# Block one of a fused scan, gated unit and squared-ReLU kernel: state copies moved to ScalarE, tiles passed whole, two tiles as three products

## The chip, the cores and the metric

The kernel runs on one core of a Trainium2 chip. The metric is the device time of one launch, in microseconds (us), as the median of three runs. A core has TensorE (PE: matrix products, with its weight loads shown apart as PEld), VectorE (DVE), ScalarE (ACT), GpSimd (POOL), and SyncE (SP), which here only issues transfers. Each engine takes its own instructions strictly in the order in which they were issued to it, and waits on semaphores for the others.

## The reference

Three stages follow each other. A state-space scan over 4 x 8 heads of 768 steps, in chunks, then a gated unit, then a squared-ReLU layer:

```python
# scan, per chunk (log_a is summed within the chunk to cum)
y = (C B^T * exp(cum_i - cum_j) * causal) x + (C state) * exp(cum)
state = exp(sum) * state + sum_j B_j x_j exp(cum_end - cum_j)
# gated unit on 3072 tokens of 256, d_ff 1536
xn = x / sqrt(mean(x * x) + 1e-6) * rms_g
x = (silu(xn @ w_gate) * (xn @ w_val)) @ w_out
# squared ReLU, d_ff 2048
out = (s * relu(x @ w_in) ** 2 + b) @ w_out2
```

## The kernel before

**Work and its names.** The 3072 tokens are 32 *units* of 96 tokens (`UT`), worked on in pairs. For a pair, `scan` spreads the decays over partitions with PE (tile `ab`) and scans them on DVE (`a_sb`), `gram` multiplies B and C on PE (tile `y`) and masks the result on DVE (`m`), `outs` makes y from `m` and `xh` on PE, squares it on ScalarE (`xn`, with its row sums in `ss`), raises the sums to the power -1/2 on GpSimd (`rs`) and scales y on ScalarE (`xn` again), and `turn` transposes `xn` on PE and copies it out, scaled by `rms_g`, as `xth` (and, from block two on, its remainder `xtl`). `keep_state` copies the state rows of a unit (16 x 256) into `xh` of the unit two further on, which needs them for its own y.

**The gated unit** takes the units in seven *blocks*; block one (`j == 0`) is 4 units, 384 columns. The 1536 hidden features are 12 weight tiles (`F1`). Tiles come as the raw words of the array (`raw`) and are decoded to `w1f` by `decode`: on DVE `e`, the masked `raw`, a `SCALAR_TENSOR_TENSOR` into `w1f`, the product of `e` and `sg`, and the last product into `w1f`; on ScalarE `sg` and the exponent `e`. From block two on a product is *three products*: weights and data are split into a high part (`w1h`, `xth`, `hi`: a copy on ScalarE) and the rest (`w1l`, `xtl`, `lo`: a subtraction on DVE), and high*high, low*high, high*low are summed, each a fast pass. Block one has the *plain* form: `hidden1_plain` takes the float32 tile `w1f` as it is, in four-pass products. It does so half by half: half 0 is the columns of the first pair of units, half 1 those of the second pair. Half 0 of tiles runs while the second pair is still in the scan; half 1 follows three tiles behind (`behind`). A half is 4 products into one bank of `h` (gate and value side by side), a Silu on ScalarE, a product on DVE (both into the small tile `h`), and, two halves later (`LAG`), 2 products into the sums `o`.

**What sets the order.** Nothing is issued as it is written. `Plan` records every operation, prices it, schedules it (`forward`, `backward`), and issues each engine's operations in the order of the planned starts. Where the plan has TensorE idle before 34 us (`AWAKE`), `issue` fills the gap with small products of ones (line 354; "fills" below). All other instructions are issued at line 361, so the rows below are told apart by their tiles. Transfers go out on SyncE in the planned order; at most eight are under way.

Of the kernel before, what the change touches and what calls it, by code (L numbers as in the profile page):

```python
# [40 lines left out]
F1 = 12  # L41
F2 = 16
N2 = 512
HALF = N2 // 2
# [13 lines left out]
class Plan:  # L58
# [7 lines left out]
    SEM_OF = {"tensor": 0.26}  # L66
    DMA_LEAD, DMA_TAIL, DMA_ISSUE, DMA_RATE = 1.7, 1.3, 0.55, 270e3
    DMA = {"sync": "dma", "scalar": "dma0"}
# [14 lines left out]
    def __init__(self, nc):  # L83
        self.nc, self.ops, self.clock, self.pace = nc, [], 0.0, False
        self.seen, self.rings, self.masks, self.before, self.heads = {}, {}, {}, {}, {}
        self.closed, self.sent, self.turns, self.bundle = set(), None, False, None
        self.now_free, self.floor, self.latest = True, None, None
        self.fresh, self.after, self.held, self.squares = False, None, None, None
        for e in ("tensor", "vector", "scalar", "gpsimd", "sync"):
            setattr(self, e, Engine(self, e))  # L90
# [76 lines left out]
    def touch(self, op, ap, write):  # L167
        t = getattr(ap, "tensor", None)
        tag = getattr(t, "tag", None)
        if tag is None:  # L170
            return
        tag = str(tag)
        name = ap.name
        whole = "PSUM" in str(ap.space) or "DRAM" in str(ap.space)
        if name not in self.seen:
            self.seen[name] = []
            ring = self.rings.setdefault(tag, [])
            bufs = t.bufs or t.tag_meta.bufs
            self.before[name] = list(self.seen[ring[-bufs]]) if len(ring) >= bufs else []
            self.closed.update(ring[:1 - bufs] if bufs > 1 else ring)  # L180
            ring.append(name)
        for *_, o in self.before[name]:
            self.need(op, o)
        p0, p1, mask = (0, 128, self.banks(ap)) if whole else self.cover(ap)
        for w, q0, q1, m, o in self.seen[name]:
            if (write or w) and q0 < p1 and p0 < q1 and m & mask:
                self.need(op, o)
        assert name not in self.closed, name
        self.seen[name].append((write, p0, p1, mask, op))
# [10 lines left out]
    def price(self, eng, fn, args, kw):  # L200
# [4 lines left out]
        if fn == "dma_start":  # L205
            return max(0.06, out.nbytes() / self.DMA_RATE)
        if eng == "tensor":
# [11 lines left out]
        if eng == "vector":  # L219
# [6 lines left out]
            return (n / (1.92 if fast else 0.96) + 67 + more) / 1e3  # L226
        if fn == "tensor_tensor":
            return 0.9 if self.now_free else 2.0
        return n / 1.15e3 + (0.25 if fn == "affine_select" else 0.06)
# [9 lines left out]
    def forward(self, succs, late):  # L239
# [15 lines left out]
        for _ in ops:  # L255
# [24 lines left out]
            if e in ("dma", "dma0"):  # L280
                done = carried = max(now + self.DMA_LEAD, carried) + op["dur"]
                flights.append(done + 0.85)
# [93 lines left out]
def scan_glu_relu2(ctx: ExitStack, tc: tile.TileContext, bc, xr, aa, cst, w1, w2, gn, sv, bv, out):  # L376
# [33 lines left out]
    warm = const.tile([P, 1], F32, name="warm")  # L410
    held = const.tile([P, NPAIR], F32, name="held")
    a_scr = dram.tile([2 * NUNIT, NH * AW], F32, name="a_scr")

    w1h = [wts.tile([P, 6, P], F32R, tag="w1h", name="w1h") for m in range(F1)]
    w1f, w1l, w2f, w2h = {}, {}, {}, {}
# [157 lines left out]
    def keep_state(c):  # L573
        for z in range(2):
            t = z ^ c % NPAIR
            copy = nc.scalar.copy if c >= NPAIR else nc.vector.tensor_copy
            copy(out=x_t[c + NPAIR][z * R:z * R + NST], in_=rows_of(c)[t * R:t * R + NST])

    def outs(units):
# [28 lines left out]
        nc.gpsimd.tensor_tensor(out=rs, in0=ss, in1=mhalf.to_broadcast([P, NPAIR]), op=ALU.pow)  # L608
        if units[0] == 0:

            nc.vector.tensor_copy(out=held, in_=rs)
            nc.held = len(nc.ops) - 1
        for c in units:
# [20 lines left out]
    def turn(units):  # L634
        for c in units:
            j = BLOCK[c]
            if c == FIRST[j]:
                xt_h[j] = xt_p.tile([P, 2, NB[j]], F32R if j else F32, tag="xth", name="xth")
                if j:
                    xt_l[j] = xt_p.tile([P, 2, NB[j]], F32R, tag="xtl", name="xtl")  # L640
        bundled("t", units, turn_products)
        for c in units:
            j, p = BLOCK[c], c % NPAIR
            step = steps_of(j, p).index(c // NPAIR)
            tp = y_t.pop(c)[:, 1, 4 * R:4 * R + 2 * P].rearrange("p (k z r) -> p k z r", k=2, z=2)
            for k in range(2):
                src = tp[:, k, :, NST:R]
                hi = columns(xt_h[j][:, k], j, p)[:, step]
                nc.scalar.activation(out=hi, in_=src, func=AF.Copy, scale=g_sb[:, k:k + 1])
                if j:  # L650
                    lo = columns(xt_l[j][:, k], j, p)[:, step]
                    nc.vector.scalar_tensor_tensor(
                        out=lo, in0=src, scalar=g_sb[:, k:k + 1], in1=f32(hi), op0=ALU.mult, op1=ALU.subtract
                    )

# [11 lines left out]

    def decode(raw, out, n):

# [16 lines left out]
        )  # L686
        nc.after, nc.held = nc.held, None
        nc.vector.scalar_tensor_tensor(
            out=out, in0=low, scalar=2.0 ** -32, in1=high, op0=ALU.mult, op1=ALU.add
        )  # L690
        pw = e.bitcast(BF16)
        nc.after = None
        nc.vector.tensor_tensor(out=pw, in0=pw, in1=sg, op=ALU.mult)
        nc.vector.tensor_tensor(out=out, in0=out, in1=pw, op=ALU.mult)

# [14 lines left out]
    def decode1(m):  # L710
        if m not in raw1:
            load1(m)
        raw = raw1.pop(m)
        w1f[m] = wlo.tile([P, 6, P], F32, tag="wlo", name="w1f")
        decode(raw, flat(w1f[m]), 6 * P)

    def split1(m):
        w1l[m] = wlo.tile([P, 6, P], F32R, tag="wlo", name="w1l")
        split(flat(w1f.pop(m)), flat(w1h[m]), flat(w1l[m]))


    def decode2(m):
        raw = w2_p.tile([P, 4 * P], I64, tag="w2", name="raw2")
        words(raw, w2[m])
        w2f[m] = w2f_p.tile([P, 4, P], F32, tag="w2f", name="w2f")
        decode(raw, flat(w2f[m]), 4 * P)
        if m:
# [11 lines left out]

    def split(src, hi, lo):  # L740
        nc.scalar.copy(out=hi, in_=src)
        nc.vector.tensor_tensor(out=lo, in0=src, in1=f32(hi), op=ALU.subtract)

# [5 lines left out]
    def out1(j, m, hi, lo):  # L749
        if m == 0:  # L750
            o_t[j, 1] = new_o()
        o = [t[:, :NB[j]] for t in o_t[j, 1]]
        for t in range(2):
            three(o[t], w1h[m][:, 4 + t, :], w1l[m][:, 4 + t, :], hi, lo, m == 0, m == F1 - 1)
            if m == F1 - 1:
                evac1(o, t, j)
# [13 lines left out]
    def hidden1(j, m):  # L770
        gv = []
        for v in range(2):
            ps = ps_h.tile([P, 512], F32, tag="h", name="h")[:, :NB[j]]
            for k in range(2):
                three(ps, w1h[m][:, 2 * k + v, :], w1l[m][:, 2 * k + v, :],
                      xt_h[j][:, k], xt_l[j][:, k], k == 0, k == 1)
            gv.append(ps)
# [8 lines left out]
    def hidden1_plain(j, m, half):  # L786
        n = NB[j] // 2
        cols = slice(half * n, (half + 1) * n)
        ps = ps_h.tile([P, 512], F32, tag="h", name="h")[:, :2 * n].rearrange("p (v n) -> p v n", v=2)
        for v in range(2):  # L790
            for k in range(2):
                nc.pace = True
                nc.tensor.matmul(out=ps[:, v], lhsT=w1f[m][:, 2 * k + v, :],
                                 rhs=xt_h[j][:, k, cols], start=k == 0, stop=k == 1)
                nc.pace = False
        s = hl_p.tile([P, n], F32, tag="hi", name="h32")
        nc.scalar.activation(out=s, in_=ps[:, 0], func=AF.Silu)
        nc.vector.tensor_tensor(out=s, in0=ps[:, 1], in1=s, op=ALU.mult)

        def out():  # L800
            o = [t[:, :NB[j]] for t in o_t[j, 1]]
            last = m == F1 - 1
            for t in range(2):
                nc.pace = True
                nc.tensor.matmul(out=o[t][:, cols], lhsT=w1f[m][:, 4 + t, :], rhs=s,
                                 start=m == 0 and half == 0, stop=last and half == 1)
                nc.pace = False
                if last and half:
                    evac1(o, t, j)
        pending.append(out)  # L810
# [219 lines left out]
    for i in range(F1 + behind):  # L1030
        if i < F1:
            decode1(i)
            hidden1_plain(0, i, 0)
            drain(LAG)
        tokens_to(count[1] + (count[3] - count[1]) * (i + 1) // behind if i < behind else
                  count[3] + (count[7] - count[3]) * (i + 1 - behind) // F1)
        if i >= behind:
            hidden1_plain(0, i - behind, 1)
            drain(LAG)
# [3 lines left out]
    for layer, j in phases:  # L1043
        plan += [(layer, j, m) for m in range(F1 if layer == 1 else F2)]
    start = {(layer, j): i for i, (layer, j, m) in reversed(list(enumerate(plan)))}
    marks = [(start[1, j], count[FIRST[j] + BLOCKS[j] - 1]) for j in range(1, NBLK)]
    for i, (layer, j, m) in enumerate(plan):
        if (layer, j) == (1, 1):
            split1(m)
        if layer == 1 and 2 <= j < NBLK - 1 and m % 3 == 0:  # L1050
            nc.floor = nc.latest
            decode2((j - 2) * 4 + m // 3)
            nc.floor = None
        late = m if layer == 1 and j == NBLK - 1 else F1 + m // 2 if (layer, j) == (2, 0) and m % 2 == 0 else None
        if late == 0:
# [91 lines left out]
```

## Time and profile before

| | |
|---|---|
| median of 3 runs | 632.26 us (632.1 to 632.53) |
| profiled execution, its own time | 632.08 us |
| its span, first to last instruction | 630.1 us |
| TensorE busy | 620.6 us, 98% of the span |
| VectorE / ScalarE / GpSimd busy | 484.1 / 445.5 / 50.6 us |
| mean granted TensorE clock | 0.998 of full speed |

The span is what the trace shows; the device time is 1.98 us more than it in this execution. TensorE's busy share counts the fills as well. A product in float32 leaves two records per instruction, so "x8" of the plain form is four products.

### The profile page before, as it was taken

The numbers are of one execution on the slowest core, as the hardware profiler recorded it, in microseconds if no ns is written. First come the engines' busy times: TensorE is split into PE (matmuls) and PEld (weight loads), VectorE is DVE, ScalarE is ACT, GpSimd is POOL, SyncE is SP. The second block draws the span as 40 slices with busy tenths as digits, with TensorE's granted clock in tenths as the row PEclk, the third lists the DMA queues.
The fourth block names the chain that finished last, engine by engine and source line by source line (L and its number), as shares of the span: only waits on it lengthen the run. The fifth ranks groups of instructions, "written<-read, shape, count | busy, mean of one in ns | idle before, by whom it ended". The sixth has DMA issues, their size and how long they took to land.

```text
span 630.1 us, 13021 instructions
## 1 busy us (share of the span) xinstructions
PE 620.6 (98%) x4997; PEld 554.8 (88%) x4997; DVE 484.1 (77%) x980; ACT 445.5 (71%) x940; POOL 50.6 (8%) x88
## 2 busy tenths in 40 slices
PE   8999999999999999999999999999999999999996
PEld 7899999999988888888888889999999999999986
DVE  7999955777657756757775568798897897987975
ACT  4788435666545546654655579899898999988985
POOL 3000000000101111101232220000000000000000
PEclk9999999999999999999999999999999999999999
DMA  7887203344313422400100000001010010010101
GB/s 225 208 265 236 56 5 69 76 96 99 106 34 90 111 78 62 126 14 8 36 2 1 1 1 1 2 2 33 1 34 2 1 34 1 8 28 1 34 1 34
DMA packets 33694, 35.00 MB, mean 56 GB/s; under 512 B 14048, under 2 KB 30048, under 8 KB 33632
## 3 DMA queue, kind: packets, MB, share of 16 engines
q1 hardware_dynamic: 32688, 33.71, 20.7%
q8 instruction: 39, 0.64, 0.4%
q10 hardware_dynamic: 944, 0.46, 0.2%
q14 instruction: 23, 0.19, 0.1%
HBM read 30.90 MB, written 3.25 MB: 54 GB/s over the span
## 4 chain that ended last, share of the span: by engine, by line
PE 93%; DVE 2%; DMA 2%; ACT 1%; SPq 1%; issue 0%; DVEq 0%
PE h L361 54%; PE o L361 22%; PE acc L361 13%; PE y L361 5%; DMA raw<-in_w 1%; SPq L361 1%; DVE w1f L361 0%; DMA first_bc<-in_bc 0%; DVE res L361 0%; DVE e L361 0%; ACT xn L361 0%; DVE a_sb L361 0%; ACT e L361 0%; DVE raw L361 0%; ACT xth L361 0%
## 5 line engine op out<-in xcount | busy, mean ns | idle before, releaser
L361 ACT CAST hi<-s 128x256 fp32r<-128x256 f32 (+2 forms) x168 | 79.1, 474 | 71.1 <-DVE s L361 69.0
L361 ACT ACTIVATE s<-h 128x512 f32<-128x512 f32 (+2 forms) x168 | 96.1, 572 | 36.0 <-PE h L361 33.0
L361 PE MATMUL h<-x1h,w2h 128*128 128x512 f32 x384 | 119.2, 391 | 0.0
L361 DVE TENSOR_TENSOR lo<-s,hi 128x256 fp32r<-128x256 f32 (+2 forms) x168 | 85.8, 511 | 30.0 <-ACT hi L361 27.2
L361 PE MATMUL h<-xtl,w1h 128*128 128x480 f32 (+1 forms) x288 | 106.7, 371 | 0.0
L361 PE MATMUL h<-xth,w1l 128*128 128x480 f32 (+1 forms) x288 | 106.5, 370 | 0.0
L361 PE MATMUL h<-xth,w1h 128*128 128x480 f32 (+1 forms) x288 | 106.2, 369 | 0.3
L361 PE MATMUL acc<-hi,w2c 128*128 128x256 f32 x448 | 81.9, 281 | 0.0
L361 PEld LDWEIGHTS h<-x1h,w2h 128*128 128x128 f32 x384 | 69.2, 188 | 12.3
L361 DVE TENSOR_TENSOR s<-h,s 128x480 f32<-128x480 f32 (+1 forms) x72 | 44.6, 620 | 43.9 <-PE h L361 43.6
L361 PE MATMUL h<-x1l,w2h 128*128 128x512 f32 x192 | 75.0, 390 | 0.0
L361 PEld LDWEIGHTS acc<-hi,w2c 128*128 128x128 f32 x448 | 71.0, 189 | 2.2
L361 DVE TENSOR_TENSOR added<-s 128x256 f32<-128x256 f32 x144 | 56.5, 420 | 13.5 <-ACT s L361 12.5
L361 PE MATMUL acc<-lo,w2c 128*128 128x256 f32 x224 | 63.1, 282 | 0.0
L361 ACT ACTIVATE s<-s 128x512 f32<-128x512 f32 x96 | 60.2, 632 | 1.9
L361 PEld LDWEIGHTS h<-xth,w1h 128*128 128x128 f32 x288 | 54.1, 188 | 7.4 <-DVE s L361 1.1
L361 PEld LDWEIGHTS h<-xtl,w1h 128*128 128x128 f32 x288 | 54.1, 188 | 6.3 <-issue 1.0
L361 PEld LDWEIGHTS h<-xth,w1l 128*128 128x128 f32 x288 | 54.0, 188 | 6.4 <-issue 0.5
L361 PE MATMUL o<-lo,w1h 128*128 128x480 f32 (+1 forms) x144 | 53.0, 368 | 0.0
L361 PE MATMUL o<-hi,w1l 128*128 128x480 f32 (+1 forms) x144 | 52.9, 367 | 0.0
L361 PE MATMUL o<-hi,w1h 128*128 128x480 f32 (+1 forms) x144 | 52.9, 367 | 0.0
L361 DVE TENSOR_TENSOR lo<-added,hi 128x768 fp32r<-128x768 f32 x48 | 45.9, 957 | 0.5 <-ACT hi L361 0.5
(98 smaller groups left out, 1090.6 us busy)
## 6 DMA issues: line engine op xcount, KB each, us to landing
raw<-in_w SPq DMA_DIRECT2D x12, 768.0 KB, 5.5
raw<-in_w SPq DMA_DIRECT2D x16, 512.0 KB, 3.4
a_sb<-a_scr SPq DMA_DIRECT2D x28, 196.0 KB, 4.2
xh<-in_xr SPq DMA_DIRECT2D x60, 48.0 KB, 1.9
raw_bc<-in_bc SPq DMA_DIRECT2D x56, 32.0 KB, 2.4
raw_bc<-in_bc SPq DMA_DIRECT2D x112, 16.0 KB, 3.2
out_t<-res SPq DMA_DIRECT2D x13, 96.0 KB, 2.0
out_t<-res SPq DMA_DIRECT2D x5, 144.0 KB, 1.9
```

Source lines behind the costliest of these rows:

```text
L361: getattr(engine, op["fn"])(*op["args"], **op["kw"])
```

## The change

- `keep_state` copies all states on ScalarE. Before, those of the first pair were copied on DVE. They now stand behind the squares of the same unit on the same engine. `held`, a copy that kept DVE's decode behind `rs`, is gone.
- Block one is passed in halves only for tiles 0 to 2 (`HALVES`). Tiles 3 to 9 are passed whole: 384 columns in one product, gate and value in two banks.
- Tiles 10 and 11 (`PLAIN` and up) are split at once (`split1`), and in block one they run as three products. For that `xth` of block one is split into a high part in the `res` buffer and a remainder `xtl0`. The blocks after it take the tiles in the order 10, 11, 0, ..., 9 (`ORDER`), since those two have been split.
- The planner's prices for transfers change, and it now orders any two engines that touch one PSUM tile. So the order of everything changes.

```diff
+PLAIN = 10
+HALVES = 3
+ORDER = [*range(PLAIN, F1), *range(PLAIN)]
...
-    DMA_LEAD, DMA_TAIL, DMA_ISSUE, DMA_RATE = 1.7, 1.3, 0.55, 270e3
+    DMA_LEAD, DMA_TAIL, DMA_ISSUE, DMA_RATE = 1.7, 0.75, 0.45, 270e3
+    DMA_BEGIN, DMA_LATER, DMA_THIN = (10.0, 0.68), 1.15, 1.1
...
-            if (write or w) and q0 < p1 and p0 < q1 and m & mask:
+            apart = "PSUM" in str(ap.space) and o["eng"] != op["eng"]
+            if (write or w or apart) and q0 < p1 and p0 < q1 and m & mask:
...
-            copy = nc.scalar.copy if c >= NPAIR else nc.vector.tensor_copy
-            copy(out=x_t[c + NPAIR][z * R:z * R + NST], in_=rows_of(c)[t * R:t * R + NST])
+            nc.scalar.copy(out=x_t[c + NPAIR][z * R:z * R + NST], in_=rows_of(c)[t * R:t * R + NST])
...
-            nc.vector.tensor_copy(out=held, in_=rs)
...
-        cols = slice(half * n, (half + 1) * n)
-        ps = ps_h.tile([P, 512], F32, tag="h", name="h")[:, :2 * n].rearrange("p (v n) -> p v n", v=2)
+        cols = slice(0, NB[j]) if half is None else slice(half * n, (half + 1) * n)
+        if half is None:
+            ps = [ps_h.tile([P, 512], F32, tag="h", name="h")[:, :NB[j]] for v in range(2)]
+        else:
+            both = ps_h.tile([P, 512], F32, tag="h", name="h")
+            ps = [both[:, v * n:(v + 1) * n] for v in range(2)]
...
             decode1(i)
-            hidden1_plain(0, i, 0)
-            drain(LAG)
+            if i < HALVES:
+                rows0 = xt_h[0]
+                hidden1_plain(0, i, 0)
+                drain(LAG)
+            if i >= PLAIN:
+                split1(i)
...
+        if i - behind == PLAIN:
+            xt_h[0] = res_p.tile([P, 2, NB[0]], F32R, tag="res", name="xth0")
+            xt_l[0] = [w2f_p.tile([P, NB[0]], F32R, tag="w2f", name="xtl0") for k in range(2)]
+            for k in range(2):
+                split(rows0[:, k], xt_h[0][:, k], xt_l[0][k])
         if i >= behind:
-            hidden1_plain(0, i - behind, 1)
+            if i - behind < PLAIN:
+                hidden1_plain(0, i - behind, 1 if i - behind < HALVES else None)
+            else:
+                hidden1(0, i - behind)
             drain(LAG)
```

The first place at which the order moves is DVE after the first pair's masks (`m`), where the first weight tile's decode begins. Before:

```order
L361 COPY xh<-y 16x256
L361 TENSOR_SCALAR e<-raw_137 128x768
L361 COPY xh<-y 16x256 x2
L361 TENSOR_SCALAR raw_137<-raw_137 128x768
L361 TENSOR_SCALAR ss<-ss 128x2
L361 COPY xh<-y 16x256
L361 SCALAR_TENSOR_TENSOR a_sb<-ab,delta 128x392
L361 TENSOR_TENSOR e<-e,sg 128x768
L361 COPY held<-rs 128x2
L361 SCALAR_TENSOR_TENSOR w1f<-raw_137 128x768
```

And now:

```order
L370 TENSOR_SCALAR e<-raw_136 128x768
L370 TENSOR_SCALAR raw_136<-raw_136 128x768
L370 TENSOR_SCALAR ss<-ss 128x2
L370 SCALAR_TENSOR_TENSOR w1f<-raw_136 128x768
L370 TENSOR_TENSOR e<-e,sg 128x768
L370 TENSOR_SCALAR e<-raw_137 128x768
L370 TENSOR_TENSOR w1f<-w1f,e 128x768
L370 SCALAR_TENSOR_TENSOR a_sb<-ab,delta 128x392
```

The four copies and `held` have left DVE, and the scan `a_sb` of the second pair stands behind the first tile's decode. From here to the second pair's `ss` DVE had 33 instructions before and has 23 now; besides the copies, the last step of tile 2 and three of tile 3's decode and a product `h` now come behind that `ss`.

The second place is the second pair's way to `xth`. ScalarE before, from the square of the pair's first unit on:

```order
L361 ACTIVATE xn,ss<-y 128x256
L361 COPY xh<-y 16x256 x2
L361 ACTIVATE xn,ss<-y 128x256
L361 ACTIVATE sg<-raw_188 128x768
L361 ACTIVATE h_173<-h 128x192
L361 COPY xh<-y 16x256 x2
L361 ACTIVATE xn<-y,rs 128x256 x2
L361 ACTIVATE e<-e,fixed 128x768
L361 ACTIVATE h_185<-h 128x192
L361 ACTIVATE xth<-y,sb 128x96 x4
```

And now, from the square of its second unit on (`raw_179` is weight tile 3, `h_172` half 0 of tile 2):

```order
L370 ACTIVATE xn,ss<-y 128x256
L370 ACTIVATE sg<-raw_179 128x768
L370 ACTIVATE e<-e,fixed 128x768
L370 ACTIVATE xn<-y,rs 128x256 x2
L370 COPY xh<-y 16x256 x2
L370 ACTIVATE h_172<-h 128x192
L370 ACTIVATE xth<-y,sb 128x96 x2
L370 ACTIVATE sg<-raw_185 128x768
L370 ACTIVATE xth<-y,sb 128x96 x2
```

TensorE before, around the transposes `y<-ident,xn` of that pair (`h_164`, `h_173`, `h_185` are half 0 of tiles 1, 2, 3):

```order
L361 MATMUL h<-xth,w1f 128x192 x3
L361 MATMUL o_133<-h_164,w1f 128x192
L361 MATMUL o_134<-h_164,w1f 128x192
L361 MATMUL h<-xth,w1f 128x192 x4
L361 MATMUL y<-ident,xn 128x128 x4
L361 MATMUL o_133<-h_173,w1f 128x192
L361 MATMUL o_134<-h_173,w1f 128x192
L361 MATMUL h<-xth,w1f 128x192 x8
```

And now (`h_163`, `h_172` are half 0 of tiles 1, 2; 26 fills stand ahead of the first row):

```order
L370 MATMUL h<-xth,w1f 128x192 x4
L370 MATMUL y<-ident,xn 128x128 x4
L370 MATMUL o_132<-h_163,w1f 128x192
L370 MATMUL o_133<-h_163,w1f 128x192
L370 MATMUL o_132<-h_172,w1f 128x192
L370 MATMUL h<-xth,w1f 128x192 x8
L370 MATMUL o_133<-h_172,w1f 128x192
```

The transposes stand behind three half tiles instead of four, and behind them come the second halves of tiles 0 and 1 (`x8`). Four fills follow, then half 1 of tile 2, and from there whole tiles.

The third place is DVE at the end of block one. Now (`raw_245` is tile 11, the last one; the first `w1l` is that of tile 10, the next that of tile 11):

```order
L370 TENSOR_TENSOR w1f<-w1f,e 128x768
L370 TENSOR_SCALAR e<-raw_245 128x768
L370 TENSOR_TENSOR h_259<-h,h_259 128x384
L370 TENSOR_SCALAR raw_245<-raw_245 128x768
L370 TENSOR_TENSOR w1l<-w1f,w1h 128x768
L370 SCALAR_TENSOR_TENSOR w1f<-raw_245 128x768
L370 TENSOR_TENSOR e<-e,sg 128x768
L370 TENSOR_SCALAR ss<-ss 128x2
L370 TENSOR_TENSOR w1f<-w1f,e 128x768
L370 TENSOR_TENSOR s<-h,s 128x384
L370 TENSOR_TENSOR w1l<-w1f,w1h 128x768 x2
```

Before, the first `w1l` of any tile stood behind the last decode, and was wanted by block two alone; now two of them are wanted by block one. Of all fills 129 stood in the order before, 105 now.

## Rows read from the trace of the kernel before

**Rows 1.** The page's first part: busy time, share of the span and instructions by engine.

```profile
PE 620.6 (98%) x4997; PEld 554.8 (88%) x4997; DVE 484.1 (77%) x980; ACT 445.5 (71%) x940; POOL 50.6 (8%) x88
```

**Rows 2.** Stretches: length, busy us (instructions) PE PEld DVE ACT POOL, clock, DMA.

```profile
16.08:31.44 15.36, 14.51 (x214) 12.62 (x214) 15.12 (x30) 11.70 (x27) 1.33 (x1) 1.00 0.81 211
31.44:75.86 44.42, 44.23 (x440) 42.62 (x441) 43.60 (x86) 32.88 (x73) 2.59 (x2) 1.00 0.68 198
...
140.00:600.00 460.00, 459.98 (x3281) 404.89 (x3280) 350.15 (x710) 339.38 (x701) 38.15 (x55) 1.00 0.13 33
```

**Rows 3.** Groups on TensorE up to 31.44 us: records | busy us, mean ns | idle.

```profile
L361 PE MATMUL h<-xth,w1f 128*128 128x192 f32 x32 | 6.7, 344 | 0.7 <-DVE w1f L361 0.7
...
L361 PE MATMUL o<-h,w1f 128*128 128x192 f32 x12 | 2.4, 326 | 0.0
```

**Rows 4.** Timeline of TensorE: start, us, what, [idle before <-releaser].

```profile
8.02 1.90 PE L361 MATMUL y<-xh,m 64*64 64x32 f32 x64
...
16.08 1.54 PE L361 MATMUL h<-xth,w1f 128*128 128x192 f32 x8 [0.74 <-DVE w1f L361]
...
17.55 1.06 PE L361 MATMUL y<-first_bc 16*64 16x64 f32 x64
...
31.44 2.87 PE L361 MATMUL h<-xth,w1f 128*128 128x192 f32 x16 [0.60 <-ACT xth L361]
```

**Rows 5.** The chain that ended last: start, us, what.

```profile
34.96 1.30 PE h L361 x8
...
84.86 2.12 PE h L361 x12
```

**Rows 6.** Timeline of ScalarE, columns as in rows 4.

```profile
9.67 0.38 ACT L361 ACTIVATE xn<-y 128x256 f32<-128x256 f32 x1 [7.45 <-DVE xh L361]
...
21.14 0.92 ACT L361 ACTIVATE sg<-raw 128x768 bf16<-128x768 int16 x1 [1.07 <-DMA raw<-in_w]
...
27.70 0.33 ACT L361 ACTIVATE h<-h 128x192 f32<-128x192 f32 x1
28.06 0.73 ACT L361 COPY xh<-y 16x256 f32<-16x256 f32 x2
28.82 0.84 ACT L361 ACTIVATE xn<-y,rs 128x256 f32<-128x256 f32 x2
...
30.58 1.04 ACT L361 ACTIVATE xth<-y,sb 128x96 f32<-128x96 f32 x4
```

**Rows 7.** Timeline of VectorE, columns as in rows 4.

```profile
21.66 0.96 DVE L361 TENSOR_TENSOR_SCAN a_sb<-ab,delta 128x392 f32<-128x392 f32 x1
...
22.99 0.74 DVE L361 TENSOR_TENSOR m<-y,a_sb 128x384 f32<-128x384 f32 x2
23.66 0.95 DVE L361 TENSOR_TENSOR w1f<-w1f,e 128x768 f32<-128x768 f32 x1
...
24.72 0.55 DVE L361 TENSOR_SCALAR raw<-raw 128x768 int32<-128x768 int32 x1
25.19 0.55 DVE L361 TENSOR_TENSOR e<-e,sg 128x768 bf16<-128x768 bf16 x1
25.66 0.95 DVE L361 SCALAR_TENSOR_TENSOR w1f<-raw 128x768 f32<-128x768 uint32 x1
26.52 0.35 DVE L361 TENSOR_TENSOR h<-h,h 128x192 f32<-128x192 f32 x1
27.04 0.17 DVE L361 TENSOR_SCALAR ss<-ss 128x2 f32<-128x2 f32 x1 [0.17 <-ACT xn L361]
...
62.35 0.94 DVE L361 TENSOR_TENSOR w1f<-w1f,e 128x768 f32<-128x768 f32 x1
```

**Rows 8.** Transfers issued by SyncE: start, us, what.

```profile
7.95 3.83 SPq L361 DMA_DIRECT2D first_bc<-in_bc  x4
...
15.40 0.35 SPq L361 DMA_DIRECT2D raw<-in_w  x1
```

**Rows 9.** Transfers issued up to 31 us: count, KB each, median us to landing.

```profile
first_bc<-in_bc SPq DMA_DIRECT2D x8, 62.0 KB, 5.2
```

## What was predicted, with its working

> **What bounds the kernel now.** I read the page's busy shares first, then stretches of the run, then the timeline around the moments at which TensorE stops waiting. TensorE is busy in 98% of the span [rows 1], and from 31.44 us on it is simply full: 44.23 of the 44.42 us up to 75.86, and 459.98 of the 460 us from 140 to 600, all at a granted clock of 1.00, the 2.4 GHz level [rows 2]. So the end of this kernel is the moment at which TensorE becomes full, plus the work that it has left then. What an edit is worth is read as: how much earlier does the full stretch begin, and how much work lies in it.
>
> The full stretch begins at 31.44 us, after a wait for ScalarE's `xth` [rows 4]: the second pair's columns of block one have arrived, and from there every decoded tile can be multiplied twice. Until then TensorE has only half 0 of the tiles. Its records up to 31.44 are 32 of `h` and 12 of `o` [rows 3]; with two records per product that is 4 half tiles of hidden products and 3 half tiles of output products. The rest of that time is the scan's products, fills and waits.
>
> What holds `xth` back is a chain through four engines: masks on DVE, y on TensorE, squares on ScalarE, `ss` on DVE at 27.04 [rows 7], scaling on ScalarE at 28.82 [rows 6], transposes, and `xth` from 30.58 [rows 6]. Two things stretch it. In the first pair the square waits for DVE's state copy and starts only at 9.67, with ScalarE idle for 7.45 us ahead of it [rows 6], though the first half of the y products, 8.02 plus half of 1.90, is over at about 9.0 [rows 4]. And DVE, in order and 15.12 of 15.36 us busy from 16.08 to 31.44 [rows 2], has decode work in front of the masks.
>
> **The start of the full stretch, now.** I follow the changed order, with durations from rows. A price on DVE is the distance from one start to the next, since neighbours overlap by about 0.09 us: 0.86 for a 768-column product or `SCALAR_TENSOR_TENSOR` (25.66 to 26.52), 0.47 for a 16-bit step (25.19 to 25.66), 0.67 for the two masks of a unit (22.99 to 23.66), 0.27 for the small `h` product and 0.88 for a scan (their 0.35 and 0.96 less the overlap) [rows 7]. The masked `raw` and `e` I take as 0.47 too.
>
> The first pair: the squares follow the y products, which end at 9.92, so the first `ss` comes at about 10.5 and `xth` of half 0 some 1.2 us earlier than now; TensorE's first `h` starts at about 14.5, not 16.08 [rows 4]. This alone is worth nothing, since TensorE waits for the second pair anyway.
>
> The second pair: its B and C (`first_bc`) still queue behind the raw tiles. They were issued from 7.95 to 11.78 and land 5.2 us later [rows 8, 9], the last at about 17.0, the first unit's at about 16.6. Its products take half of 1.06 us [rows 4], so the first mask starts at about 17.3. DVE is there in time: it is free from 9.0 at the latest (the second unit's y, the second half of the 1.90 us from 8.02, waits for its masks), and the 13 instructions ahead come to 7.1 us, with about 0.6 of waiting for the squares: 16.7. From 17.3 DVE does masks, the end of tile 1 (0.86), a scan (0.88), one 0.47 step and the other unit's masks: 0.67 + 0.86 + 0.88 + 0.47 + 0.67 = 3.55, to 20.85. TensorE makes the second unit's y in 0.95 (half of 1.90 [rows 4]), to 21.9. Its square starts at 22.0, and ScalarE is free again at 22.4; `ss` comes at about 22.5, where it was at 27.04.
>
> Behind the square ScalarE has, in its order, `sg` (0.92), `e` (the same size, 0.92), two scalings (0.84), two state copies (0.73), one Silu (0.33), two `xth` (half of 1.04), `sg` (0.92) and two `xth` [rows 6]. That is 22.4 + 0.92 + 0.92 + 0.84 + 0.73 + 0.33 + 0.52 + 0.92 = 27.6 at the start of the last two, and TensorE can start on half 1 when the first of them is done, about **27.8**. GpSimd's power of `ss` lies beside `sg` and `e`; the transposes and half 0 of tile 2 lie beside the copies. So the full stretch begins 31.44 - 27.8 = 3.64 us earlier. With hand-overs 0.1 us slower at each of a dozen places it is 29.0, and with ScalarE's overlaps (its busy times are taken whole here) 27.0.
>
> **The work left then.** A plain half tile of hidden products is 8 records in 1.30 us, 0.325 a product; 12 fast products of 384 columns take 2.12, 0.177 each [rows 5].
> - Before, at 31.44: 20 half tiles of hidden products (26.0) and 21 of output products at 0.65 (13.65), 39.65 us. The stretch to 75.86 is 44.42, so 4.77 us of scan products lie in it; they stay.
> - Now, at 27.8: half 0 of only 3 tiles and 2.5 half outputs are done. Left are 3 hidden halves (3.90), 3.5 output halves (2.28), seven whole tiles at 12 x 0.325 = 3.90 (27.3), and two tiles of 18 fast products at 3.19 (6.37): 39.85.
> - Whole tiles: no row shows a float32 product of 384 columns. Four passes over 192 columns at 2.4 GHz are 0.320 of the 0.325, so joining two saves between 0 and 0.005 each, 0 to 0.2 us over 42; I take 0.
>
> So three products save 2 x 0.71 = 1.43 us, and 1.63 us that was done inside the wait now lies behind it: +0.20. The four fills between the second halves cost about 0.3. **The sum is -3.64 + 0.20 + 0.3 = -3.15 us.** From block two on nothing is taken away or added but the order of the tiles, and TensorE is full there. The profiled execution took 632.08, so 628.93; that execution lies 0.18 below the median of the runs, so on the median's scale **629.1 us**.
>
> **What is late next: DVE's remainders.** Tiles 10 and 11 need `w1l` inside block one, and DVE takes it between decodes. From `ss` at 22.6 to the end of tile 11's `w1l` its order has 21 long steps (18.1), 26 of 0.47 (12.2), 5 small and ten 384-column products (1.35 and 4.7, at 0.47 between the 0.27 and the 0.86), 4 scans (3.5), 4 pairs of masks (2.7), four `xtl` (as the small products, 1.1) and trifles (0.3): 43.9, so 66.5. Tile 10's comes 3.6 us earlier, at 62.9. TensorE, full from 27.8, asks for tile 10's at about 63.8 and for tile 11's at about 68.2. With 0.2 us for the hand-over DVE is ahead by 0.7 us at the first and 1.5 at the second. Before, DVE idled 0.82 us in the whole stretch [rows 2], so I expect no wait or a few tenths.
>
> VectorE was busy 43.60 of 44.42 us in that stretch [rows 2]. A rule speaks against the change here: the Trainium skill (Perfetto Trace Analysis, Identifying the Most-Contended Engine) takes VectorE's occupancy as a fair measure of its limit, says that the engine with the highest is to be relieved first, and distrusts matmul busy time. By that rule block one belongs to DVE, which gets four steps more. The trace disagrees so far: DVE's last decode ended at 63.2 (62.35 + 0.86 [rows 7]), and TensorE worked on for 12.6 us without it.
>
> **The rivals.**
> 1. *DVE becomes the bound of block one.* Every microsecond by which DVE comes later than above costs TensorE what exceeds 0.7. For it: the margin is thin, the engine runs in order, and whole tiles leave it less freedom (their product waits for both banks). Against it: 0.82 us of idle time before. Delays of 2 to 3.5 us leave a gain of 0.3 to 1.9: 630.3 to 632.0. This is the time that the rule gives.
> 2. *The start does not come earlier.* If the transfers hold the second pair (they moved at 211 GB/s at a share of 0.81 there [rows 2]), full work begins near 31 as before, and only the +0.5 of the other terms stands: 632 to 632.8.
> 3. *The other side: a late weight tile in ScalarE's queue.* `sg` of tile 3 stands ahead of the scaling of the second pair. Before, ScalarE stood 1.07 us waiting for just this tile, which was issued at 15.40 and had landed by 21.1 [rows 6, 8]. Now it can go out when tile 0's buffer is read, at about 12, and is wanted at 22.4. If it lands at 26.0 the gain of 3.15 is nearly gone; from 27.0 on the kernel is slower by more than 0.2%: 633.6. Against it: 5.7 us from issue to landing [rows 6, 8] would be 18.
> 4. *The clock.* 24 fills fewer stand in the order. TensorE was granted 1.00 with 0.85 us idle from 16.08 to 31.44 [rows 2]; were it at the lower level, 1.2 GHz, there, the products would take twice as long, and 4.4 us of them on the second pair's way would turn the gain of 3.15 into a loss of 1.26: 633.5.
>
> **Chances.** My forecast, a gain of 1.9 to 4.7: 0.70. Rival 1: 0.15, two thirds of it still over 1.26 us, which is the 0.2% that a measurement here can tell from no change. Rival 2: 0.08. Rivals 3 and 4: 0.05 and 0.02. So faster 0.80, within 0.2% 0.13, slower 0.07. The range runs from 627.5 (start at 27.0, whole tiles 0.2, block two without its first short waits 0.5) to 631.2, into rival 1.
>
> **What would show it.** Right: ScalarE's first square at about 9.1 without a wait for DVE; second `ss` near 22.5; TensorE full from 27 to 29; block one's last hidden products 3 us earlier than 75.9, with no gap over 0.3 us ahead of the products with `w1l`; a whole float32 product at 0.645 to 0.65. Wrong: a wait of ScalarE's `sg` for a transfer between 22 and 25; TensorE waiting for DVE between 30 and 70 by more than a microsecond in sum; a granted clock under 1.00 before 30; or TensorE short of full after block one, which I take to be unchanged.

## The result and the profile after

The changed kernel takes 635.46 us (median of 4 executions, 634.28 to 636.47) against 632.18 us for the kernel before: a ratio of 1.0051, 95% interval 1.0032 to 1.0069. It is slower, where I forecast 629.1 us. The profiled execution took 634.28 us, with a span of 632.4 us (630.1 before); it is the fastest of the four.

The page's busy times of the changed kernel, which answer to [rows 1]:

```profile
PE 622.9 (99%) x4877; PEld 544.9 (86%) x4877; DVE 481.8 (76%) x970; ACT 449.1 (71%) x939; POOL 52.1 (8%) x88
```

TensorE has 120 records fewer and is busy for 2.3 us more. The timeline of TensorE shows where, columns as in [rows 4]; `o<-const-bfloat16-1.0` are the fills:

```profile
0.77 2.61 PE L363 MATMUL o<-const-bfloat16-1.0 128*128 128x128 bf16 x23 [0.77 <-PEq L1155]
...
4.53 2.88 PE L370 MATMUL ab<-a_cl,ident 128*64 128x196 f32 x16 [1.15 <-DVE a_cl L370]
...
10.66 3.23 PE L370 MATMUL y<-xh,m 64*64 64x32 f32 x64
13.82 1.57 PE L370 MATMUL ab<-a_cl,ident 128*64 128x196 f32 x8
...
25.61 1.12 PE L370 MATMUL y<-xh,m 64*64 64x32 f32 x32
...
32.01 3.10 PE L370 MATMUL h<-xth,w1f 128*128 128x192 f32 x16
```

The first gap holds 23 fills. Behind it TensorE stands idle for 1.15 us, and its products then run at about half rate, until about 17 us: the 64 products of y with `m` take 3.23 us where they took 1.90 [rows 4]. They end at 13.89 instead of 9.92. The full stretch begins at 32.01, 0.57 us later than before and 4.2 us later than forecast. The first square on ScalarE and the two `ss` on VectorE follow (columns as in [rows 4]):

```profile
12.63 0.38 ACT L370 ACTIVATE xn<-y 128x256 f32<-128x256 f32 x1 [3.24 <-PE y L370]
```

```profile
14.45 0.17 DVE L370 TENSOR_SCALAR ss<-ss 128x2 f32<-128x2 f32 x1 [3.33 <-ACT xn L370]
...
27.29 0.17 DVE L370 TENSOR_SCALAR ss<-ss 128x2 f32<-128x2 f32 x1 [0.34 <-ACT xn L370]
```

The square waits for the y products and no longer for VectorE's copy, as intended, but stands at 12.63 and not at 9.1. The second `ss` is at 27.29, where I had 22.5 and the kernel before 27.04 [rows 7].

The stretches, columns as in [rows 2]; the first is the start, of which [rows 2] has no row:

```profile
0.77:16.08 15.31, 14.16 (x198) 11.88 (x199) 8.73 (x22) 4.36 (x9) 6.11 (x22) 1.00 0.74 222
...
32.01:75.86 43.85, 43.43 (x352) 29.80 (x351) 42.85 (x78) 34.30 (x70) 2.71 (x2) 1.00 0.65 188
140.00:600.00 460.00, 458.61 (x3270) 403.46 (x3269) 346.76 (x706) 338.77 (x699) 38.35 (x55) 1.00 0.13 33
```

Three things stand here. The clock column reads 1.00 for the start too, but there it shows no measurement. The trace keeps the granted clock as records (start, length, level), and the column counts what no record covers as 1.00. The first record of the changed kernel, at 1.00 (the 2.4 GHz level), begins at 17.29 us; that of the kernel before begins at 3.46. Ahead of it the level is to be read from the durations, and they are near those of the lower level, 1.2 GHz: the products of y with `m` take 1.7 times as long. Experiment 1 shows the same ratio in a stretch whose record reads 0.50. Block one is full: TensorE lacks 0.42 us, a wait for `xh`. And from 140 us on, where TensorE had 459.98 of 460 us, it now lacks 1.39 us. TensorE's timeline finds most of that in two places, near 147 and 163 us; the first:

```profile
146.98 0.34 PE L370 MATMUL h<-xtl,w1h 128*128 128x384 f32 x1
148.13 0.44 PE L370 MATMUL h<-xth,w1h 128*128 128x384 f32 x1 [0.82 <-DVE s L370]
```

VectorE's timeline there, of the changed kernel and below it of the kernel before:

```profile
146.66 0.97 DVE L370 TENSOR_TENSOR_SCAN a_sb<-a_sb,delta 128x392 f32<-128x392 f32 x1 [2.74 <-DMA a_sb<-a_scr]
147.55 0.53 DVE L370 TENSOR_TENSOR s<-h,s 128x384 f32<-128x384 f32 x1
```

```profile
144.74 0.56 DVE L361 TENSOR_TENSOR s<-h,s 128x384 f32<-128x384 f32 x1 [1.39 <-PE h L361]
146.33 1.84 DVE L361 TENSOR_TENSOR_SCAN a_sb<-a_sb,delta 128x392 f32<-128x392 f32 x2 [1.03 <-DMA a_sb<-a_scr]
```

Before, the product `s` stood ahead of the scan. Now the scan, which waits 2.74 us for its transfer, stands ahead of `s`, and TensorE waits for `s` to free a bank. From product to product the two places cost 1.15 and 0.91 us where a slot is 0.18: 0.97 and 0.73 us. So the span's 2.3 us are 0.57 of a later start and 1.70 of these waits.

### The profile page after: what moved, and what is told of

Its sections match the earlier page's. It is cut to its first block, busy times and chain, and to the rows that moved or that the text cites. A ratio compares the mean times of both kernels' runs of the same rounds, so it can differ in the third digit from the quotient of the medians.

```text
span 632.4 us, 12785 instructions
## 1 busy us (share of the span) xinstructions
PE 622.9 (99%) x4877; PEld 544.9 (86%) x4877; DVE 481.8 (76%) x970; ACT 449.1 (71%) x939; POOL 52.1 (8%) x88
## 4 chain that ended last, share of the span: by engine, by line
PE 90%; DVE 6%; ACT 2%; issue 1%; DMA 1%; POOL 0%; DVEq 0%; SPq 0%; ACTq 0%; POOLq 0%
PE h L370 50%; PE o L370 20%; PE acc L370 13%; PE y L370 6%; DVE w1f L370 1%; DVE e L370 1%; PE ab L370 1%; PE o L363 1%; DMA a_sb<-a_scr 1%; DVE raw L370 1%; DVE w1l L370 0%; DVE h L370 0%; DVE a_sb L370 0%; ACT xh L370 0%; ACT sg L370 0%
## 5 line engine op out<-in xcount | busy, mean ns | idle before, releaser
L370 PE MATMUL h<-xth,w1h 128*128 128x480 f32 (+1 forms) x296 | 108.6, 369 | 1.4 <-DVE s L370 1.4
L370 PE MATMUL h<-xth,w1l 128*128 128x480 f32 (+1 forms) x296 | 109.3, 369 | 0.0
L370 PE MATMUL h<-xtl,w1h 128*128 128x480 f32 (+1 forms) x296 | 109.1, 370 | 0.0
L370 PEld LDWEIGHTS h<-xth,w1h 128*128 128x128 f32 x296 | 55.6, 188 | 8.5 <-DVE s L370 2.4
L370 PEld LDWEIGHTS h<-xtl,w1h 128*128 128x128 f32 x296 | 55.6, 188 | 6.4 <-issue 1.2
L370 PEld LDWEIGHTS h<-xth,w1l 128*128 128x128 f32 x296 | 55.5, 188 | 6.2 <-issue 0.3
L370 PE MATMUL o<-hi,w1l 128*128 128x480 f32 (+1 forms) x148 | 54.2, 366 | 0.0
```

Source lines behind the costliest of these rows:

```text
L370: getattr(engine, op["fn"])(*op["args"], **op["kw"])
```

## The experiments

None of these kernels leaves out a part of the computation. A median stands with the range of the executions. "Theory A" is the clock at the start.

**1. The fills of the first gap, given back to the changed kernel** (30; then 36):

```diff
                     fills += 1
                     busy += self.FILL * (2 if busy < self.CHILL else 1)
+                while fills < 30:
+                    self.nc.tensor.matmul(
+                        out=idle, lhsT=ones, rhs=ones, start=not fills, stop=True, skip_group_check=True
+                    )
+                    fills += 1
```

> The changed kernel with 30 fills ahead of the first scan product instead of 23, everything else in the same order. Theory A (the clock: with seven fills fewer TensorE stood idle for 1.15 us ahead of its first products and then ran at about half rate until 17 us): the first 16 products of the scan take about 1.55 us again, not 2.88, the y products behind m about 1.9, not 3.23, the second pair's ss comes at 22.5 to 23.5 instead of 27.29, the full stretch begins near 28 instead of 32.0, and the time is 630.0 to 631.5; what is left above my forecast are the two stalls in block three. Rival B (the late start comes from the new order on ScalarE and DVE, not from the clock): the products keep their lengths or the full stretch still begins at 31.5 to 32, and the time stays at 634 to 636.5.

> The changed kernel with 36 fills ahead of the first scan product. Theory A: TensorE has already been brought to the higher level by about 30, so six more only fill the wait for the clipped a; the same as the run with 30 within 0.4 us, 630.0 to 631.5. If the rate falls again through the remaining idle gap ahead of the products, this run is faster than that with 30 by up to a microsecond. Rival B: 634 to 636.5.

Measured: 637.21 us (631.44 to 638.08) with 30, ratio 1.0069 (1.0044 to 1.0094), and 637.07 (632.10 to 639.25) with 36. Neither theory foresaw this. The first half of A holds: the 64 products of y with `m` take 1.90 us again, and the first `ss` comes at 11.13, where the changed kernel has 14.45. (The 16 products of `ab` still take 2.20, for the clock records begin at 5.90, among them.) But the second `ss` comes at 27.54, and TensorE's timeline with 30 fills shows a new stop:

```profile
4.54 2.20 PE L375 MATMUL ab<-a_cl,ident 128*64 128x196 f32 x16 [0.41 <-issue]
...
19.39 1.06 PE L375 MATMUL y<-xh,m 64*64 64x32 f32 x29
22.21 0.30 PE L375 MATMUL y<-xh,m 64*64 64x32 f32 x3 [1.77 <-issue]
22.44 2.45 PE L375 MATMUL h<-xth,w1f 128*128 128x192 f32 x8
```

The engine stops within a unit's 32 products, for nothing that a semaphore shows ("issue"), and behind the stop it runs at half rate (2.45 us for eight records that take 1.30 to 1.57 elsewhere); the granted clock is 0.50 from 22.97 to 26.38 us. With 36 fills the same place reads:

```profile
19.14 0.88 PE L375 MATMUL y<-xh,m 64*64 64x32 f32 x23
22.82 0.64 PE L375 MATMUL y<-xh,m 64*64 64x32 f32 x9 [2.80 <-issue]
...
26.89 1.92 PE L375 MATMUL y<-xh,m 64*64 64x32 f32 x32
```

and the stretch around it, columns as in [rows 2]:

```profile
21.87:32.11 10.24, 9.29 (x78) 8.55 (x78) 4.32 (x9) 5.10 (x13) 1.56 (x1) 0.50 0.69 171
```

Here the granted clock is recorded as 0.50, the 1.2 GHz level, and 32 products of y with `m` take 1.92 us where they take 1.12 elsewhere. That is the ratio of the changed kernel's start, 1.7. So a stop can cost, besides its own length, a stretch at the lower level behind it.

Six fills more ahead of it, and the stop comes six products earlier: after TensorE's 347th record of a product in both. That ties it to the count of instructions and not to an operand; experiment 4 tests it. (A float32 product counts as two here, one for each record.) The run with 36 fills also stops after its 221st; the two lie 126 products, with their weight loads 252 records, apart. One of the queues that carry instructions (q8) has 38 packets, 0.62 MB in all, so 16 KB each, and the DMA view of the run with 30 fills shows none of them from 13 to 19.6 us and one from 19.6 to 20.75:

```profile
q1 hardware_dynamic: 955, 1.25, 72.2%
```

```profile
q1 hardware_dynamic: 261, 0.27, 122.8%
q8 instruction: 1, 0.02, 5.5%
```

Its packet ends at 20.71 and TensorE goes on at 22.21; with 36 fills at 21.32 and 22.82, 1.50 us each time. The Trainium skill (Runtime: NRT & Kernel Launch, Instruction fetch mechanics) says that an engine's instructions come in blocks of 16 KiB, 256 instructions, over a queue of their own, and that the cost is mostly hidden. Size and distance agree. That the cost is hidden does not hold at this start.

The spread of the executions fits. One execution of each run lost little against the kernel before, 631.44 and 632.10 us; its mean granted clock is 0.999. The others have 0.989 to 0.997 and take 635.05 us and more.

**2. The kernel before with 23 fills in its first gap**, the rest as it was (`and not (fills == 23 and first)` in the condition of the loop).

> The kernel before with only 23 of its 30 fills ahead of the first scan product, everything else in the same order. Theory A (the clock at the start): the same half rate up to about 17 us as in the changed kernel, a later second ss and a full stretch from 33 to 36, so 634 to 637. Rival B (order, not clock): seven fills in an idle wait are worth nothing, 632.0 to 632.5.

Measured: 635.43 us (632.79 to 635.54), ratio 1.0047 (1.0030 to 1.0064), as A expected. TensorE's timeline has the start of the changed kernel to a hundredth, and a full stretch from 35.81; the trace's clock records begin only at 19.08 us:

```profile
4.53 2.88 PE L361 MATMUL ab<-a_cl,ident 128*64 128x196 f32 x16 [1.15 <-issue]
...
10.66 3.23 PE L361 MATMUL y<-xh,m 64*64 64x32 f32 x64
...
35.81 2.87 PE L361 MATMUL h<-xth,w1f 128*128 128x192 f32 x16 [0.59 <-ACT xth L361]
```

Seven fills in an idle wait are worth 3.0 us to the kernel before by the ratio, 3.6 between the medians. One of the four executions (632.79) hardly lost; experiment 6 comes back to that.

**3. The prices of transfers apart from the structure.** First the changed structure with the prices of before, then the kernel before with the new ones:

```diff
-    DMA_LEAD, DMA_TAIL, DMA_ISSUE, DMA_RATE = 1.7, 1.3, 0.55, 270e3
+    DMA_LEAD, DMA_TAIL, DMA_ISSUE, DMA_RATE = 1.7, 0.75, 0.45, 270e3
+    DMA_BEGIN, DMA_LATER, DMA_THIN = (10.0, 0.68), 1.15, 1.1
...
-                done = carried = max(now + self.DMA_LEAD, carried) + op["dur"]
+                begin = max(now + self.DMA_LEAD, carried)
+                done = carried = begin + op["dur"] * (self.DMA_BEGIN[1] if begin < self.DMA_BEGIN[0] else self.DMA_LATER)
```

> The changed kernel with its transfers priced as in the kernel before: all changes of structure stay (ScalarE's copies, whole tiles, three products, the order of tiles), while the planner puts 30 fills in the first gap again and keeps the order of the scan's transfers and products from which the stalls at 147 and 163 us came away. Theory A with the second loss from the prices: a fast start, full from about 28, no wait of TensorE for DVE's product s near 147 and 163, 629.0 to 630.5. Rival C (the structure costs: whole tiles, three products or DVE's copies of work in block one): 632 or more, with the loss between 32 and 76 us.

> The kernel before with the new prices of transfers alone, and at least 30 fills in the first gap as it had; no copies on ScalarE, no whole tiles, no three products. Theory P (the order that the new prices give at the start sets transfers, and TensorE's own instruction blocks, late): slower than before by 2 to 6 us, 634 to 638, with TensorE stopped or at half rate before 32 us. Rival C (the prices are harmless at the start, the structure costs): 631.5 to 632.5.

Measured: 631.17 us (629.33 to 632.98), ratio 0.9995 (0.9984 to 1.0006), and 635.08 us (632.55 to 640.44), ratio 1.0045 (1.0024 to 1.0066). So the structure costs nothing that can be measured (C falls), though the first is slower than A's range: its second `ss` comes at 26.5 and its full stretch begins at 30.5, not near 28. The order that the new prices give costs 3 us without any of the structure. Neither has waits for `s` over 0.2 us, though, so these waits are not the prices' alone. Both show a stop after TensorE's 221st or 220th product: 0.85 us with the old prices, with the granted clock at 0.50 from 14.64 to 18.05, and in the second kernel, whose profiled execution was its slowest, 3.36 us:

```profile
13.33 1.11 PE L357 MATMUL o<-const-bfloat16-1.0 128*128 128x128 bf16 x16
17.81 0.69 PE L357 MATMUL o<-const-bfloat16-1.0 128*128 128x128 bf16 x9 [3.36 <-issue]
```

There the 16 products of `ab` took 2.88 us too, the clock records begin at 8.88, and behind the stop the clock is at 0.50 from 19.12 to 29.36. Its mean granted clock is 0.991 and that of the other nine executions 0.997 or more, so where those lose their 3 us is not shown.

**4. Fewer instructions for the same busy time.** Four bfloat16 fills become one float32 product, two records in place of four. It takes about as long: the second gap's 15 fills last 0.98 us from their start to the next product's, and their stand-in (three float32 products and three fills) 1.03.

```diff
+        wide = self.nc.const_aps.tensor(1.0, (P, P), F32)
...
+                n = max(n, 30) if first else n
+                first = False
+                for one in [wide] * (n // 4) + [ones] * (n % 4):
+                    self.nc.tensor.matmul(
+                        out=idle, lhsT=one, rhs=one, start=not fills, stop=True, skip_group_check=True
+                    )
```

> The changed kernel with 30 bfloat16 fills' worth ahead of the first scan product, and everywhere four bfloat16 fills replaced by one float32 product of the same tile, which takes four passes: TensorE is as busy as with 30 fills but has some 45 instructions pairs less up to 24 us. Theory F (in the runs with 30 and 36 fills TensorE stopped at its 347th product, for want of instructions that a transfer brought late): the stop at the second pair's y goes or is under 0.5 us, the second ss is at 23 to 24, the full stretch begins at 28 to 29, 630 to 632. Rival T (what is late is late in time, not by the count of instructions: the stop comes at 20 to 25 us at another product, over 1.5 us): 634 to 638.

Measured: 631.47 us (630.86 to 632.68), ratio 0.9991 (0.9982 to 1.0000): 5.7 us less than with 30 bfloat16 fills and the same order of work. The stop is gone, the second `ss` is at 24.04, and the timeline of TensorE has

```profile
4.53 1.59 PE L376 MATMUL ab<-a_cl,ident 128*64 128x196 f32 x16 [0.21 <-issue]
...
19.49 1.12 PE L376 MATMUL y<-xh,m 64*64 64x32 f32 x32
20.54 1.57 PE L376 MATMUL h<-xth,w1f 128*128 128x192 f32 x8
...
22.36 1.12 PE L376 MATMUL y<-xh,m 64*64 64x32 f32 x32
...
28.77 3.12 PE L376 MATMUL h<-xth,w1f 128*128 128x192 f32 x16
```

This is the start that I forecast, 1 us later. F stands: fewer instructions at the same busy time took the stop away, which a delay by time alone (T) would not.

**5. The scans behind `s`.** On top of it, and then on the changed kernel alone, each scan from 100 us of the plan on is issued up to 1.6 us later in VectorE's order:

```diff
+            if op["fn"] == "tensor_tensor_scan" and 100 < start[i]:
+                when[i] = max(start[i], min([start[i] + 1.6] + [start[u] - 0.01 for u, _ in succs[i]]))
```

> The kernel with float32 fills, and from 100 us of the plan on each scan stands up to 1.6 us later in VectorE's order, so that the product s goes first; TensorE's and SyncE's orders are the same. Theory: TensorE's two waits for s near 147 and 163 us go, 1.2 to 1.7 us less than the kernel with float32 fills alone. Rival: the scan is then late for the masks and the y products wait instead, no difference within 0.4 us.

> The changed kernel, its 23 bfloat16 fills untouched, with the scans alone later in VectorE's order. It prices the second loss in the kernel as changed: 1.2 to 1.7 us less than it, 633.8 to 634.3, with full work still from about 32 us and no wait for s near 147 and 163 us. Rival: other waits take their place and it stays within 0.4 us of 635.5.

Measured: 629.75 us (628.50 to 630.61), ratio 0.9962 (0.9950 to 0.9975), 1.72 us less than without it, and TensorE's stretch is full again:

```profile
140.00:600.00 460.00, 460.00 (x3224) 405.27 (x3224) 348.52 (x706) 342.00 (x705) 37.73 (x55) 1.00 0.13 33
```

On the changed kernel alone: 632.08 us (629.91 to 634.07). That is more of a gain than expected, but its executions spread over 4 us, and the profiled one (633.78 us, full from 32.52) is only 0.5 below that of the changed kernel. From the start of the full stretch to the end it is 1.1 us shorter, with one wait for `s` of 0.3 us left. So what the scans cost the kernel as changed is bounded only loosely.

**6. Controls.** The kernel before with both repairs; the changed structure with both repairs and the old prices; both repairs with the first pair's copies back on VectorE; and both repairs with the first gap cut to 23 fills' worth (`n = 23 if first else n`).

> A control: the kernel before with the two repairs of the last run, float32 fills and scans later in VectorE's order from 100 us on; none of the change in it. If the last run's gain of 2.3 us is the change's own, this kernel stays where it was, 631.5 to 632.6, since it had no stop for instructions and no wait for s. If the repairs alone make it, this one is at 630 or less.

> The changed structure with the transfers priced as before, float32 fills and scans later. With bfloat16 fills this order gave 631.2, with a stop of 0.85 us at the 221st product and 1.75 us of waits ahead of the first h. Theory F: the stop goes; the second pair's order in it (second masks at 23.1, second ss at 26.5 us) stays, so the gain is less than a microsecond: 630.2 to 631.2. Should the prices of before be simply the better ones: under 629.5.

> The best kernel so far (float32 fills, scans later) with the first pair's four state copies back on VectorE, ahead of the squares. My prediction's reading: the first pair's earlier ss alone is worth nothing, but VectorE has four small steps more and ScalarE four less; the second ss comes 0 to 1.5 us later and the time is 629.7 to 631.5. Rival: the copies are the change's whole gain, 632 or more.

> The best kernel (float32 fills, scans later) with the fills ahead of the first scan product cut to what 23 bfloat16 ones take, as the changed kernel had them; nothing else differs. Theory A: TensorE idles 1.1 us ahead of the first products, they run at half rate (16 in 2.88 us), the second ss is 2.5 to 3.5 us later than with 30 and the time 2 to 4 us more, 631.8 to 633.8. Rival (only the stop for instructions matters): 629.5 to 630.3.

Measured: 631.95 (ratio 0.9996, 0.9986 to 1.0006), 630.17 (0.9968, 0.9956 to 0.9981), 631.39 (629.87 to 635.04) and 630.92 us (629.79 to 634.44). The first says that the gain of 2.4 us in experiment 5 is the change's own. The second lost its stop at the 221st product, and 1.0 us with it. The third is inconclusive: the second `ss` came at 25.95, but the plan also put y products ahead of `ab`. The fourth misses A's range: five executions lie at 629.8 to 630.4 and five at 631.5 to 634.4. Its profiled one (630.03 us) idled ahead of the first products like the changed kernel, yet came to full rate at about 8 us:

```profile
4.53 2.88 PE L380 MATMUL ab<-a_cl,ident 128*64 128x196 f32 x16 [0.96 <-issue]
7.34 1.35 PE L380 MATMUL y<-first_bc 16*64 16x64 f32 x64
8.62 0.93 PE L374 MATMUL o<-const-float32-1.0 128*128 128x128 f32 x6
```

Its clock records begin at 7.95 us, and an execution that reaches the higher level so early loses little. Over all profiled executions they begin at 3.46 to 8.88 us with 30 fills, their worth or more (ten kernels), and with 23 at 17.29 (the changed kernel), 19.08 (experiment 2), 19.01 (the scans alone) and here 7.95. So 23 fills do not always cost 3 us. That the slower five stayed at half rate for longer would fit, but only one execution is profiled.

## Why the prediction was wrong

| kernel | clock records from | second `ss` | full from | from there to the end | median |
|---|---|---|---|---|---|
| before | 3.46 | 27.04 | 31.44 | 598.7 | 632.2 |
| changed | 17.29 | 27.29 | 32.01 | 600.4 | 635.5 |
| 30 fills | 5.90 | 27.54 | 32.28 | 601.4 | 637.2 |
| float32 fills | 4.65 | 24.04 | 28.77 | 600.1 | 631.5 |
| and scans later | 6.47 | 24.39 | 29.12 | 598.6 | 629.8 |

(The fifth column is the span less the fourth; a median is that of all executions, the others are of the profiled one. With 30 fills the stop and the lower level behind it, experiment 1, come on top.)

- **The step that failed is "The start of the full stretch, now", 27.8 us; it was 32.01.** It took every duration on TensorE from rows at the higher level. The y products were priced at 1.90 us and to end at 9.92; they took 3.23 and ended at 13.89. With the work in the same order at full rate the full stretch begins 2.9 to 3.2 us earlier than in the changed kernel, so that the level is about 3 of the 4.2 us. The order of the steps was right: where TensorE ran at full rate and had its instructions, the second `ss` came at 24.0 to 24.4 and the full stretch at 28.8 to 29.1, at the late end of the bounds that I gave it (29.0).
- **Rival 4 named the mechanism, the lateness (4.4 us) and the side, and had 0.02.** It looked for half rate from 16.08 to 31.44 us, and I dismissed it by the granted clock there. That was a true measure, but of the kernel before and of the wrong place: the fills went missing ahead of the first products, and the half rate lay ahead of 17.29. I counted 24 fills fewer in sum, not the seven fewer in the first gap, and priced them at nothing; experiment 2 prices them. Its 633.5 us is no hit all the same, since 1.70 us of the loss have another cause, told next. The Trainium skill (TensorE: Matmul & The Clock Gate, Seeing it yourself) warns that clock events in a trace have been unreliable. This trace does not bear that out: the records, 17.29 and 7.95 us among them, begin where the products change their length, and what misled was the column's 1.00 where there is no record. For the same reason the sign that I had named, a granted clock under 1.00 before 30 us, could not show there.
- **The sentence "TensorE is full there", of all that follows block one, was wrong by 1.70 us.** I looked there for changes of work and not of order. The order on VectorE moved too, and an in-order engine with a scan waiting for its transfer held up `s`. Experiment 5 shows it.
- **Instructions were not in the sum at all.** In the changed kernel no such stop shows: held back at half rate until 17.29, it comes to its 347th product only after 24 us, and the block that was late in experiment 1 had landed at 21.46. Given its fills back, it lost the gain to the stop instead.
- **Right:** VectorE is not the bound of block one (rival 1). In 32.01 to 75.86 it is busy for 42.85 of 43.85 us and TensorE waits for it nowhere; tile 10's `w1l` ends at 68.8 and is first used at 69.7, a margin of 0.9 us for my 0.7. By the rule of the Trainium skill (Perfetto Trace Analysis, Identifying the Most-Contended Engine) VectorE would have been the limit; the trace disagrees again, since TensorE, 43.43 us busy there, never waits for it. Rivals 2 and 3, held by transfers, did not come: ScalarE's `sg` waits for none near 22 us, and with both repairs the start is 2.3 us earlier.
- **A whole float32 product is 0.645 us**, as taken: four start at 40.91 and what follows at 43.49, in TensorE's timeline of the changed kernel:

```profile
40.91 2.74 PE L370 MATMUL h<-xth,w1f 128*128 128x384 f32 x8
43.49 0.81 PE L370 MATMUL o<-h,w1f 128*128 128x192 f32 x4
```

- **The +0.50 of work left and fills does not show:** from the full stretch to the end it is 598.6 us with both repairs and 598.7 before. With that the sum closes for the profiled execution: 628.93 + 4.21 + 1.70 - 0.50 = 634.34, where it took 634.28.

With what went wrong at the start and near 147 and 163 us repaired, the change gives 629.75 us, 0.65 above the forecast and inside its range. What stays open is why a block of instructions comes so late: in the run with 30 fills TensorE reached its 221st product at about 14.2 us, and the next block's packet started only at 19.7, though the transfers had almost paused between 15 and 16 us. Nor is it shown what decides how soon an execution leaves the lower level (7.95 to 19.08 us with 23 fills), so the 3.3 us by which the changed kernel is slower are split for its profiled execution alone (2.3 us).

## What to carry to other kernels

Before an edit's gain is summed from rows, see which level of TensorE's clock each row was taken at (ahead of the trace's first clock record, by the lengths of like products and not by the clock column), and whether the edit shortens the work, fills included, ahead of the first products on the path. A plan's prices are part of the kernel: changing them reorders stretches that no edit names, so the order of the engines that wait there is to be compared from end to end. A start that issues hundreds of small products can be bound by the arrival of its instructions; here fewer, longer fills took that bound away, and they cost the kernel before nothing (631.95 us with both repairs).

## What the hardware showed that I had not expected

TensorE, busy for 14.16 of 15.31 us from 0.77 on, stayed at the lower level until 17.29 us in the changed kernel (16 products of `ab`: 2.88 us against 1.55 in the kernel before), with seven fills fewer than a kernel that left it at 3.46. TensorE stopped for 0.85 to 3.36 us with no wait that the profile shows, after its 220th or 221st product in three kernels and after its 347th in two, and went on 1.3 to 1.5 us after a 16 KB packet of instructions had landed. Behind the last stop of each of these four kernels the granted clock fell to 0.50, until 18.05, 26.38, 29.36 and 32.11 us. And executions of one program lay up to 8 us apart (632.55 to 640.44), where those of the kernel before lay within 2.8 us (631.32 to 634.12); one of each is profiled, so where the others differ is known only by their mean granted clock.
